# Gated attention and linear attention on one core: waits ordered by expected arrival, gate rows by DMA, a serial DMA queue in the build-time scheduler, the last round in two halves

## The chip, the cores and the metric

One core of one Trainium2 chip. The time is the device time of one execution in microseconds (us). The span is the time from the first to the last instruction in the profile; it is about 2 us shorter than the time (677.7 against 679.8 us in before's profiled run). All kernels below gave correct results.

## The reference

In short (both attentions are named here and not written out):

```python
def reference(A_x, A_wqkv, A_wo, B_x, B_wqkv, B_wo, gate_w):   # x: 1 x 2048 x 512, bf16
    x = A_x
    g = sigmoid((x * gate_w).sum(-1, keepdims=True))
    a = softmax_attention(x, A_wqkv, A_wo)      # branch A: 32 heads of 16, 2048 x 2048 scores
    b = linear_attention(x, B_wqkv, B_wo)       # branch B: phi(t) = where(t > 0, t+1, exp(t)) + 1e-6
    return g * a + (1 - g) * b
```

## The kernel before

The kernel schedules itself while it is built. A list scheduler holds a modelled duration for each operation and decides the order on each of the five engines; the instructions are then emitted in that order with semaphore waits. TensorE (PE) computes score blocks into PSUM banks (`ps<-Qz,KT`, three matmuls a group). Two of the three banks go to ScalarE (ACT), which takes the exponential of 128x1024 elements (`P<-ps`, 695 of them). The third goes to VectorE (DVE), which makes an approximate exponential by bit operations (`Z<-ps`, with shifts on DVE and GpSimd). PE multiplies both with V (`ps<-P,Vc`, `ps<-Z,Vc`: PV). Branch B and the projections are woven in between. Branch B's own exponentials on ACT write `eb` (32 of them); its normalised output (`OBn` in the program, `wA` in the profiles) is transposed by DMA (`xnat<-wA`) before the output matmuls read it. At the end of a round the attention output is transposed and normalised into `OAT`, which the output matmuls also read.

How waits are attached (the first of the list ends on the instruction, the others on EventSemaphore instructions ahead of it):

```python
    def add(self, fn, deps=(), inc=True, dma_sem=None):     # class _Eng
        waits = []
        for d in deps:
            if d is None:
                continue
            # ... semaphore and value of d; skipped if already waited for
                waits.append((sem, val))
```

How a DMA is modelled: the issue holds SP for 60 ns and the data land a fixed latency later, however many DMAs stand before it.

```python
        def dma(E, o, i, sem, total, lat, ..., issue=60.0):
            start = max(E.free, _avail(E, reads, writes))
            E.free = start + issue
            fin = start + lat
```

The loads at the start, the gate, and V's blocks:

```python
        for t in range(1, NQC):
            for cc in range(NCC):
                dma(SP, xT[...], x2[...], semXT[t], ..., transpose=True, issue=1300.0)     # 12 transposes
            # ... one weight load after t == 1
        dma(SP, gwc[:], gate_w.rearrange("(cc p) -> p cc", p=128), semG, 16, 3000.0, ...)  # 1 KB
...
            # a block of V: one eviction, then two scaled copies on GpSimd
            yield dv(607, lambda: nc.vector.tensor_copy(Vc[:, 0, vs, :, :, 0:16], src), [r_bank[b]], [r_V[vs]])
            for k in range(1, NTERM):
                yield po(690, lambda k=k: nc.gpsimd.tensor_scalar(Vc[:, k, vs]..., COEF[k], ...), [r_V[vs]], [r_V[vs]])
...
        def t_gate():
            yield po(900, lambda: nc.gpsimd.tensor_copy(gwr, gwc[:]...to_broadcast(...)), [r_gw], [r_gwr])
            # ... gate matmuls, sigmoid ...
            for a in range(4):          # gate rows: a strided copy per 32 partitions
                yield dv(150, lambda ...: nc.vector.tensor_copy(gnat[32 * a:32 * (a + 1), :], src), [r_ge], [r_gnat])
```

The softmax here doesn't subtract the row's maximum and nothing guards it: scores larger than these inputs give would overflow.

## Time and profile before

| | before |
|---|---|
| time, median of 3 runs | 680.0 us (679.25 to 680.65) |
| span of the profiled run | 677.7 us |
| first exponential starts / last one ends | 9.93 / 669.47 us |
| median distance between starts of exponentials | 904 ns |
| ACT time lost over that pace | 15.9 us |

The last row is the sum, over all consecutive exponentials, of the distance of their starts minus 904 ns (and minus 477 ns more where an `eb` activation lies between them). With the same exponentials at the same pitch, the time can fall only if such losses go, or if the head before the first exponential or the tail after the last gets shorter. The profile lines that carry this are in the prediction.

### The profile page before, as it was taken

The numbers are of one execution on the slowest core, as the hardware profiler recorded it, in microseconds if no ns is written. First come the engines' busy times: TensorE is split into PE (matmuls) and PEld (weight loads), VectorE is DVE, ScalarE is ACT, GpSimd is POOL, SyncE is SP. The second block draws the span as 40 slices with busy tenths as digits, with TensorE's granted clock in tenths as the row PEclk, the third lists the DMA queues.
The fourth block names the chain that finished last, engine by engine and source line by source line (L and its number), as shares of the span: only waits on it lengthen the run. The fifth ranks groups of instructions, "written<-read, shape, count | busy, mean of one in ns | idle before, by whom it ended". The sixth has DMA issues, their size and how long they took to land.

```text
span 677.7 us, 24102 instructions
## 1 busy us (share of the span) xinstructions
PE 667.5 (98%) x9886; PEld 203.2 (30%) x9886; DVE 607.9 (90%) x1062; ACT 658.2 (97%) x734; POOL 550.1 (81%) x611
## 2 busy tenths in 40 slices
PE   8999999999999999999999999999999999999998
PEld 4322233323223232222333322232332332222222
DVE  6999999998899998999899888899998988899996
ACT  5899999999999999999999999999999999999995
POOL 3767878888878888888897888898788997887882
PEclk9999999999999999999999999999999999999999
DMA  6430001200000000000002000001020021000000
GB/s 133 135 89 8 4 2 35 69 9 3 2 10 1 10 2 2 10 2 2 12 3 65 10 10 1 10 18 22 7 34 9 14 48 31 17 16 11 26 17 32
DMA packets 27963, 15.96 MB, mean 24 GB/s; under 512 B 19792, under 2 KB 26832, under 8 KB 27856
## 3 DMA queue, kind: packets, MB, share of 16 engines
q1 hardware_dynamic: 26512, 13.91, 8.1%
q8 instruction: 79, 1.29, 0.8%
q10 hardware_dynamic: 1344, 0.52, 0.3%
q14 instruction: 28, 0.23, 0.1%
HBM read 6.69 MB, written 2.10 MB: 13 GB/s over the span
## 4 chain that ended last, share of the span: by engine, by line
PE 77%; ACT 13%; issue 5%; DVE 4%; DMA 0%; POOL 0%; ACTq 0%; DVEq 0%; POOLq 0%
PE ps L371 59%; PE ps L377 18%; ACT P L771 11%; DVE Z L685 2%; ACT eb L1056 1%; DMA xnat<-wA 0%; DVE T L1021 0%; DVE gnat L1013 0%; DVE QT L957 0%; DVE wA L1163 0%; PE ps L899 0%; DVE Z L749 0%; DVE OAT L1048 0%; POOL Z L739 0%; DVE rec L1040 0%
## 5 line engine op out<-in xcount | busy, mean ns | idle before, releaser
L771 ACT ACTIVATE P<-ps 128x1024 bf16<-128x1024 f32 x695 | 645.6, 1118 | 5.9 <-PE ps L371 5.8
L739 POOL TENSOR_TENSOR Z<-Z,mcon 128x512 int32<-128x512 int32 x465 | 480.0, 1056 | 81.9 <-DVE Z L685 49.4
L685 DVE TENSOR_SCALAR Z<-ps 128x512 int16<-128x512 f32 x659 | 441.2, 684 | 53.3 <-PE ps L371 45.7
L371 PE MATMUL ps<-Z,Vc 128*17 128x512 bf16 x1977 | 282.4, 382 | 0.2
L371 PE MATMUL ps<-Qz,KT 32*128 32x512 bf16 x2048 | 272.2, 384 | 3.4 <-DVE Z L685 1.0
L371 PE MATMUL ps<-P,Vc 128*17 128x512 bf16 x1389 | 250.1, 383 | 0.2
L371 PEld LDWEIGHTS ps<-Qz,KT 32*128 32x128 bf16 x2048 | 68.5, 91 | 259.1 <-ACT P L771 235.1
L371 PEld LDWEIGHTS ps<-Z,Vc 128*17 128x17 bf16 x1977 | 63.8, 88 | 79.4 <-issue 52.3
L749 DVE TENSOR_SCALAR Z<-Z 128x1024 int16<-128x1024 int16 x195 | 81.2, 433 | 0.2
L371 PEld LDWEIGHTS ps<-P,Vc 128*17 128x17 bf16 x1389 | 56.3, 88 | 55.4 <-issue 40.7
L371 PE MATMUL ps<-warm 128*32 128x512 bf16 (+15 forms) x600 | 62.5, 327 | 1.2 <-DVE dummy L420 1.2
L377 PE MATMUL ps<-xT,wA 128*32 128x512 bf16 (+1 forms) x528 | 43.9, 376 | 0.1
L1057 POOL TENSOR_SCALAR eb<-eb 128x512 f32<-128x512 f32 x32 | 20.1, 629 | 15.6 <-ACT eb L1056 9.1
L988 POOL TENSOR_SCALAR Vc<-Vc 128x576 bf16<-128x576 bf16 x32 | 21.6, 675 | 6.9 <-DVE Vc L985 3.5
L371 PEld LDWEIGHTS ps<-warm 128*32 128x32 bf16 (+1 forms) x600 | 20.3, 96 | 18.8 <-issue 12.4
L1021 DVE STREAM_TRANSPOSE T<-ps 128x512 f32<-128x512 f32 x32 | 22.6, 708 | 2.5 <-PE ps L377 2.3
L377 PE MATMUL ps<-wA,xnat 128*32 128x512 bf16 x256 | 22.6, 382 | 1.7 <-DVE wA L1163 1.7
L1044 POOL TENSOR_TENSOR T<-T,rg 128x256 bf16<-128x256 f32 x31 | 19.5, 630 | 5.7 <-DVE Z L749 2.7
L377 PE MATMUL ps<-phiK,xnat 128*32 128x512 bf16 x256 | 23.1, 383 | 0.0
L377 PE MATMUL ps<-wA,OAT 128*32 128x512 bf16 x256 | 22.5, 382 | 0.0
L1056 ACT ACTIVATE eb<-ps 128x512 f32<-128x512 f32 x32 | 22.5, 702 | 0.0
L377 PE MATMUL ps<-wB,xT 128*32 128x512 bf16 x256 | 22.4, 381 | 0.0
(79 smaller groups left out, 279.2 us busy)
## 6 DMA issues: line engine op xcount, KB each, us to landing
Qz<-QT SPq DMA_DIRECT2D x120, 16.0 KB, 1.8
wA<-in_A_wqkv_dram SPq DMA_DIRECT2D x4, 384.0 KB, 4.6
wB<-in_B_wqkv_dram SPq DMA_DIRECT2D x4, 384.0 KB, 3.3
xnat<-in_A_x_dram SPq DMA_DIRECT2D x3, 512.0 KB, 3.7
out_dram<-outt SPq DMA_DIRECT2D x12, 128.0 KB, 1.7
wA<-in_A_wo_dram SPq DMA_DIRECT2D x1, 512.0 KB, 3.6
wA<-in_B_wo_dram SPq DMA_DIRECT2D x1, 512.0 KB, 4.6
out_dram<-wA SPq DMA_DIRECT2D x4, 128.0 KB, 1.8
```

Source lines behind the costliest of these rows:

```text
L371: return lambda: nc.tensor.matmul(o, lhsT=l, rhs=r, start=start, stop=stop, skip_group_check=sg)
L377: h = nc.tensor.matmul(o[32 * j:32 * j + 32], lhsT=l[:, 32 * j:32 * j + 32], rhs=r, start=start, stop=stop, skip_group_check=True)
L685: return C(DV, OPP, 533 * n + 74, lambda: nc.vector.tensor_scalar(o, i, ZB, 0.0, op0=ALU.add, op1=ALU.max), [r_bank[b] for b in bks], r_Z[ ...
L739: return C(PO, 400, 70 + 484 * n, lambda: nc.gpsimd.tensor_tensor(Z[:, z, 0:512 * n].bitcast(I32), Z[:, z0, 0:512 * n].bitcast(I32), mcon[ ...
L749: return C(DV, 450 if hot else 300, 69 + 134 * n, lambda: nc.vector.tensor_scalar(Z[:, z, 0:512 * n], Z[:, z0, 0:512 * n], float(m), None, ...
L771: return C(AC, 500, 427 * n + 49, lambda: nc.scalar.activation(P[:, slot, 0:512 * n], bank(b0, n), ACT.Exp, scale=ESC), [r_bank[b0 + k] fo ...
L988: yield po(690, lambda k=k: nc.gpsimd.tensor_scalar(Vc[:, k, vs].rearrange("p a b c -> p (a b c)"), Vc[:, 0, vs].rearrange("p a b c -> p ( ...
L1021: yield dv(607, lambda: nc.vector.transpose(T1[:, a, :], bank(7)), [r_bank[7]], [r_T1[a]])
L1044: yield E(340 if r == NR - 1 else 640, lambda k=k: (nc.vector if r == NR - 1 else nc.gpsimd).tensor_tensor(dst_[:, k], src[:, k, :, 0:16], ...
L1056: yield ac(480, lambda: nc.scalar.activation(eb[:, i, :], bank(b), ACT.Exp), [r_bank[b]], [r_eb[i]])
L1057: yield po(640, lambda: nc.gpsimd.tensor_scalar(eb[:, i, :], eb[:, i, :], 1.0 + 1e-6, 0.0, op0=ALU.min, op1=ALU.max), [r_eb[i]], [r_eb[i]])
```

## The change

Its intent: put the wait that is expected to end last on the instruction itself, where it is cheaper (in before's profile a score group of three matmuls ended at the earliest 460 ns after its last arrival with that wait on the instruction, and 547 ns with it on an EventSemaphore); take the four gate-row copies off VectorE; make the scheduler see that DMAs of one queue follow each other (in before's profile eight Qz copies of 16 KB held SP for 5.49 us), so that it issues urgent ones earlier; and normalise the last attention round in two halves, so that the first output tiles start sooner. Some twenty scheduler constants are tuned anew with it. Cut to its core:

```diff
-        for d in deps:
-            if d is None:
-                continue
+        for d in sorted([d for d in deps if d is not None], key=lambda d: -d.fin if isinstance(d, _Ev) else 0.0):
@@ constants (cut)
-    BACK = 1005.06
-    SHB = 4
+    BACK = 980.186
+    SHB = 2
@@ DMA model
+        q_free = [0.0]
+            if E is SP and occ:
+                q_free[0] = max(q_free[0], start) + occ
+                fin = q_free[0] - occ + lat
...
+                fin = dma(SP, ..., occ=1100.0 if tr or c.name[0] in 'WX' else 650.0)
@@ gate rows
             for a in range(4):
-                src = ge[32 * a:32 * (a + 1), :, :].rearrange(...)[:, :, a]
-                yield dv(150, lambda a=a, src=src: nc.vector.tensor_copy(gnat[32 * a:32 * (a + 1), :], src), [r_ge], [r_gnat])
+                yield ("DMA", gnat[32 * a:32 * (a + 1), :], gp[32 * a:32 * (a + 1), 16 * a:16 * (a + 1)], semGN, 64, 2500.0, [r_ge], [r_gnat], False, a == 0)
@@ last round
+            if r == NR - 1:
+                for hf in range(2):
+                    # transpose, reciprocal, two multiplies, transpose back, each on 256 columns
+                    yield ("FLAG", lambda hf=hf: flags.add(("oatl", hf)))
```

More of the change, by code (lines that the diff above doesn't have):

```diff
@@ L29, with __init__ @@
 class _Ev:
-    __slots__ = ("E", "idx")
-    def __init__(self, E, idx):
+    __slots__ = ("E", "idx", "fin")
+    def __init__(self, E, idx, fin=0.0):
         self.E = E
         self.idx = idx
+        self.fin = fin
 class _Eng:
@@ L159, in bass_gated_mix__mha_block__linear_attn_block__prompt_kernel @@
     SWITCH = 100.0
-    FILL = 0.704
+    FILL = 0.7
     HOT = 32.85
-    BACK = 1005.06
-    SHB = 4
+    BACK = 980.186
+    SHB = 2
     why = [None]
@@ L166, in bass_gated_mix__mha_block__linear_attn_block__prompt_kernel @@
     PLATE = -199.667
-    SLK = 43.219
-    DSL = 900.0
-    STICK = 45.888
+    SLK = 88.975
+    DSL = 843.776
+    STICK = 65.578
     OPP = 400
     FDL = 60
-    DENS = 0.581
+    DENS = 0.743
     AGE = 300.0
+    PEP = 148.771
+    PVD = 216
     MZ = 0.0
     MZD = 0.0
-    HOLD = 74.192
+    HOLD = 109.508
     NACT = 4
-    BIAS = 141.142
-    KEYW = 32.578
-    PVW = 1365.46
-    DTOL = 44.045
-    TTOL = 38.407
-    PKR, MTR, PQR, PQS, FR = 0.500, 9.56, 12.93, 1.804, 0.0
-    KR, KS, QR = 7.15, 1.60, 4.00
+    BIAS = 82.599
+    KEYW = 7.061
+    PVW = 511.557
+    DTOL = 186.116
+    TTOL = 37.928
+    PKR, MTR, PQR, PQS, FR = 0.404, 8.73, 13.55, 1.600, 0.0
+    KR, KS, QR = 5.59, 1.48, 4.00
     NB = 2
@@ L248, in bank @@
             return ps[:, 512 * b:512 * (b + n)]
-        PE = _Eng("pe", SEM("s_pe"), 150.0)
+        PE = _Eng("pe", SEM("s_pe"), PEP)
         AC = _Eng("act", SEM("s_act"), 115.0)
@@ L277, in bass_gated_mix__mha_block__linear_attn_block__prompt_kernel @@
         r_OAT = [[R(f"OAT{t}_{q}") for q in range(NQC)] for t in range(NT8)]
+        r_OATL = [R("OATL0"), R("OATL1")]
         r_eb = [R(f"eb{i}") for i in range(2)]
@@ L306, in deps_of, with emit @@
             return deps
-        def emit(E, dur, fns, reads=(), writes=(), name=""):
+        def emit(E, dur, fns, reads=(), writes=(), name="", more=0.0):
             if callable(fns):
@@ L312, in emit @@
             E.free = start + dur
-            fin = start + dur + E.pipe
+            fin = start + dur + E.pipe + more
             deps = deps_of(E, reads, writes)
@@ L320, in emit @@
                 ev = E.add(fn, deps if k == 0 else (), inc=(k == len(fns) - 1))
+                ev.fin = fin
                 if first is None:
@@ L333, in emit, with dma @@
             LOG.append((start, E.name, dur, name))
-            RLOG.append((E.name, dur, E.pipe, [(d.E.name, d.idx) if isinstance(d, _Ev) else ("dma", id(d.sem), d.val) for d in deps if d is not None],
+            RLOG.append((E.name, dur, E.pipe + more, [(d.E.name, d.idx) if isinstance(d, _Ev) else ("dma", id(d.sem), d.val) for d in deps if d is not None],
                          ev.idx, name, cur_mode[0] if E is PE else None))
             return fin
-        dma_eng = {}
-        def dma(E, o, i, sem, total, lat, reads=(), writes=(), transpose=False, noncontig=False, name="dma", issue=60.0):
+        q_free = [0.0]
+        def dma(E, o, i, sem, total, lat, reads=(), writes=(), transpose=False, noncontig=False, name="dma", issue=60.0, occ=0.0):
             start = max(E.free, _avail(E, reads, writes))
@@ L392, in bass_gated_mix__mha_block__linear_attn_block__prompt_kernel @@
         q_fill = [0] * NQZ
+        semGN = SEM("s_gn")
         semOB = [SEM(f"s_ob{i}") for i in range(2)]
@@ L479, in t_free @@
             return max([r_bank[b].tw] + list(r_bank[b].tr.values())) + LAT
-        DMIN = 3
+        DMIN = 4
         def ready(r, kb):
@@ L828, in after @@
                 STATS["pv"] = STATS.get("pv", 0) + 1
-            return C(PE, prio, 216, fns, reads, [r_bank[7]], after, f"PV{r} {[(w['kb'], w['name']) for _, _, w in wave]}", "col",
+            return C(PE, prio, PVD, fns, reads, [r_bank[7]], after, f"PV{r} {[(w['kb'], w['name']) for _, _, w in wave]}", "col",
                      0.25 * len(wave))
@@ L865, in pe_step @@
         def pe_step(n, cols, fns, reads, writes, mode="col"):
-            return ("OP", PE, n * (cols / 2.4 + 4), fns, reads, writes, mode)
+            return ("OP", PE, n * (cols / 2.4 + PVD - 212.5), fns, reads, writes, mode)
         def pe_thin(b, fns, reads):
@@ L1009, in t_gate @@
             yield dv(650, lambda: nc.vector.reciprocal(gt[:], ge[:]), [r_ge], [r_gt])
-            yield po(200, lambda: nc.gpsimd.tensor_scalar(ge[:], gt[:], -1.0, 1.0, op0=ALU.mult, op1=ALU.add), [r_gt], [r_ge])
+            gp = ge[:].rearrange("p q c -> p (q c)")
+            yield po(200, lambda: nc.gpsimd.tensor_scalar(gp.rearrange("p (a u) -> p a u", a=4), gt[:].rearrange("p q (c a) -> p a (q c)", a=4),
+                                                          -1.0, 1.0, op0=ALU.mult, op1=ALU.add), [r_gt], [r_ge])
             for a in range(4):
-                src = ge[32 * a:32 * (a + 1), :, :].rearrange("p q (c a2) -> p (q c) a2", a2=4)[:, :, a]
-                yield dv(150, lambda a=a, src=src: nc.vector.tensor_copy(gnat[32 * a:32 * (a + 1), :], src), [r_ge], [r_gnat])
+                yield ("DMA", gnat[32 * a:32 * (a + 1), :], gp[32 * a:32 * (a + 1), 16 * a:16 * (a + 1)], semGN, 64, 2500.0, [r_ge], [r_gnat], False, a == 0)
             yield ("FLAG", lambda: flags.add("gate"))
@@ L1020, in aout, with tr_half @@
             yield ("WAIT", lambda: r < 2 or ("aout", r - 1 - a) in flags)
-            yield dv(607, lambda: nc.vector.transpose(T1[:, a, :], bank(7)), [r_bank[7]], [r_T1[a]])
+            def tr_half(hf):
+                cs = slice(256 * hf, 256 * (hf + 1))
+                return dv(341, lambda: nc.vector.transpose(T1[:, a, cs], bank(7)[:, cs]), [r_bank[7]], [r_T1[a]])
+            if r == NR - 1:
+                yield tr_half(0)
+            else:
+                yield dv(607, lambda: nc.vector.transpose(T1[:, a, :], bank(7)), [r_bank[7]], [r_T1[a]])
             def free_acc():
-                st["acc_free"] = True
+                st["acc_free"] = r < NR - 1
                 st["pv_round"] = r + 1
@@ L1033, in aout @@
             k0 = ks[0]
+            if r == NR - 1:
+                for hf in range(2):
+                    cs, gs = slice(256 * hf, 256 * (hf + 1)), slice(8 * hf, 8 * (hf + 1))
+                    if hf:
+                        yield tr_half(1)
+                    sv = T1[:, 1, cs].rearrange("p (q d) -> p q d", d=32)
+                    yield dv(115, lambda sv=sv, gs=gs: nc.vector.reciprocal(rec[:, 1, gs], sv[:, :, 16]), [r_T1[1]], [r_rec[1]])
+                    yield dv(70, lambda gs=gs: nc.vector.tensor_tensor(rg[:, c, 1, gs], rec[:, 1, gs], gt[:, qc, gs], ALU.mult), [r_rec[1], r_gt], [r_rg[c]])
+                    yield dv(210, lambda sv=sv, gs=gs, cs=cs: nc.vector.tensor_tensor(
+                        T2[:, c, cs].rearrange("p (q h d) -> p h q d", h=2, d=16)[:, 1], sv[:, :, 0:16],
+                        rg[:, c, 1, gs].unsqueeze(2).to_broadcast([128, 8, 16]), ALU.mult), [r_T1[1], r_rg[c]], [r_T2[c]])
+                    yield dv(341, lambda cs=cs: nc.vector.transpose(OAT[:, t8, 512 * qc:512 * (qc + 1)][:, cs], T2[:, c, cs]), [r_T2[c]], [r_OATL[hf]])
+                    yield ("FLAG", lambda hf=hf: flags.add(("oatl", hf)))
+                return
             src = T1[:, k0:k0 + n, :].rearrange("p a (q d) -> p a q d", d=32)
@@ L1040, in aout @@
             yield dv(155 + 17 * n, lambda: nc.vector.reciprocal(rc, src[:, :, :, 16]), rT1, rr)
-            E = dv if r == NR - 1 else po
-            yield E(70 if r == NR - 1 else 230 + 25 * n, lambda: (nc.vector if r == NR - 1 else nc.gpsimd).tensor_tensor(rgc, rc, gv, ALU.mult), [*rr, r_gt], rrg)
+            yield po(230 + 25 * n, lambda: nc.gpsimd.tensor_tensor(rgc, rc, gv, ALU.mult), [*rr, r_gt], rrg)
             for k in range(n):
-                yield E(340 if r == NR - 1 else 640, lambda k=k: (nc.vector if r == NR - 1 else nc.gpsimd).tensor_tensor(
+                yield po(640, lambda k=k: nc.gpsimd.tensor_tensor(
                     dst_[:, k], src[:, k, :, 0:16], rgc[:, k].unsqueeze(2).to_broadcast([128, 16, 16]), ALU.mult),
@@ L1069, in t_load @@
         def t_load(k, n, dst, src, sem, lat, wr, flag):
-            yield ("DMA", dst, src, sem, 16 * n, lat, [now()], wr, False, k == 0)
+            yield ("DMA", dst, src, sem, 16 * n, lat + 1000.0, [now()], wr, False, k == 0)
             if k == n - 1:
@@ L1187, in rd @@
                 kind, i = seqk[k]
-                return [r_xn[qb], r_woB] if kind == "b" else [r_OAT[i][qc], r_woA]
+                return [r_xn[qb], r_woB] if kind == "b" else [r_OATL[qbl // 2] if tail and i == NT8 - 1 else r_OAT[i][qc], r_woA]
             for k0, k1 in ((0, 2), (2, 4), (4, 6), (6, 7)):
                 yield pe_step(k1 - k0, 512, [f(k) for k in range(k0, k1)], sum((rd(k) for k in range(k0, k1)), []), [r_bank[b]])
-            yield ("WAIT", lambda: ("oat", NT8 - 1, qc) in flags)
+            yield ("WAIT", lambda: (("oatl", qbl // 2) if tail else ("oat", NT8 - 1, qc)) in flags)
             yield pe_step(1, 512, [f(7)], rd(7), [r_bank[b]])
@@ L1200, in t_final @@
                 yield ("WAIT", lambda: qb < 2 or ("f", qb - 2) in flags)
-            if tail and qbl % 2 == 1:
+            if tail and qbl != 2:
                 yield ac(480, lambda: nc.scalar.copy(ot, bank(b)), [r_bank[b]], [r_ot])
@@ L1452, in bass_gated_mix__mha_block__linear_attn_block__prompt_kernel @@
                 _, o, i, sem, tot, lat, rd, wr, tr, chk = c.fns[1]
-                fin = dma(SP, o, i, sem, tot, lat, reads=rd, writes=c.writes, transpose=tr, name=c.name)
+                fin = dma(SP, o, i, sem, tot, lat, reads=rd, writes=c.writes, transpose=tr, name=c.name, occ=1100.0 if tr or c.name[0] in 'WX' else 650.0)
                 if not chk:
```

## The prediction

> **What bounds the kernel now.** I read the page's busy shares first, then the groups, then distances between starts on ScalarE (ACT), then a timeline around each long distance.
>
> ```profile
> PE 667.5 (98%) x9886; PEld 203.2 (30%) x9886; DVE 607.9 (90%) x1062; ACT 658.2 (97%) x734; POOL 550.1 (81%) x611
> L771 ACT ACTIVATE P<-ps 128x1024 bf16<-128x1024 f32 x695 | 645.6, 1118 | 5.9 <-PE ps L371 5.8
> PEld ps L371 <- ACT P L771: 238.2, 602, 1.2
> ```
>
> PE and ACT both look full. The third line (from the waits) decides between them: 602 times PE's weight loads wait for an exponential (L771), 238 us in all, while ACT waits for PE only 5.8 us. So PE follows ACT, through the score banks that an exponential frees. PE's 98% includes padding (matmuls on `warm`). A duration of 1118 ns is no cost either: consecutive exponentials overlap. From start to start the trace has 904 ns as the median; 461 of the 661 distances between two exponentials lie within 900 to 919 ns. An `eb` activation (32 of them) adds 477 ns.
>
> The first exponential starts at 9.9 us, the last ends at 669.5, and 8.2 us follow to the end of the span (677.7). Taking 904 or 477 ns off every distance leaves 15.9 us of lost ACT time in these 659.5 us. The page's 5.9 us is only the part in which ACT is visibly empty. With no loss at all the span would be 677.7 - 15.9 = 661.8 and, with the 2.3 us between span and measured time (680.0 - 677.7), the time 664.1. That is 2.3% under the present one, so a gain over 2% (under 666.4 us) needs nearly all the losses.
>
> I traced each late exponential to the PE group whose semaphore released it, and that group to its own last wait. The 15.9 us divide so: 8.0 us in 184 small delays where PE was busy with earlier work (44 ns each); 3.5 us in 13 cases where the score group waited for VectorE (DVE); 4.0 us in 7 cases where PV matmuls were late to free a P or bank slot; the rest are crumbs. Two cases of the second kind are large, and the change addresses both.
>
> ```profile
> 63.12 2.13 DVE L1013 COPY gnat<-ge 32x16 f32<-32x16 f32 x4
> 66.30 0.13 PEld L371 LDWEIGHTS ps<-Qz,KT 32*128 32x128 bf16 x3 [1.19 <-ACT P L771]
> 66.33 0.39 PE L371 MATMUL ps<-Qz,KT 32*128 32x512 bf16 x3 [1.04 <-DVE Z L685]
> 66.76 1.02 ACT L771 ACTIVATE P<-ps 128x1024 bf16<-128x1024 f32 x1 [0.76 <-PE ps L371]
> ...
> 552.65 3.67 SPq L352 DMA_DIRECT2D Qz<-QT  x5
> 556.36 5.19 SPq L348 DMA_TRANSPOSE xnat<-wA  x3
> 559.63 0.69 DVE L1163 TENSOR_TENSOR wA<-ps,wA 128x512 bf16<-128x512 f32 x1 [2.06 <-DMA xnat<-wA]
> 561.50 1.02 ACT L771 ACTIVATE P<-ps 128x1024 bf16<-128x1024 f32 x1 [1.66 <-PE ps L371]
> ```
>
> Columns are start, duration, engine, line, operation. Upper block: four gate-row copies hold DVE for 2.1 us where the kernel's scheduler planned 4 x 150 ns; the DVE half of a score group is late, its bank is not free, ACT starts 0.91 us late. Lower block: the issue queue on SP works through Qz copies first, so the transposes of OBn start at 556.36; DVE stands 2.06 us for one of them, ACT starts 1.77 us late.
>
> [...] the first wait in the kernel's list ends up on the instruction, the others on EventSemaphores ahead of it. [...] A three-matmul score group ends at the earliest 460 ns after its last semaphore arrives if that wait is on the matmul, and 547 ns if it is on the EventSemaphore: 87 ns dearer. [...] So "expected last placed first" moves the real wait onto the instruction.
> [...] the first two gate copies took 0.72 and 0.97 us and ended 29 and 35 ns after a GpSimd shift; the last two, with GpSimd idle, 0.17 us each.
> [...] 550.8 to 561.5 us: eight Qz copies took 5.5 us to issue, about 0.69 each; the scheduler counted 60 ns.
>
> **The change part by part.** The kernel schedules itself while it is built, so the new constants reorder PE nearly everywhere; I compared the two instruction streams. Work is nearly the same: 695 exponentials in both (before, one was half size), 2048 score matmuls, 3364 PV matmuls instead of 3366, 199 padding groups instead of 202. Shifts move slightly from DVE (195 to 187) to GpSimd (465 to 471: 6 x 1.06 = 6 us on an engine that is 81% busy, so free).
>
> - Gate rows by DMA: four DVE copies leave (2.1 us of DVE), four small SP copies come, some 0.7 us of issue each, ahead of Qz copies that have time. On the path: the 0.9 us stall at 66.8. **-0.9**.
> - Serial queue: in the new stream seven OBn transposes go out in a row before the last eight Qz copies (before: five), and the one transpose behind them is read only by the output matmuls, over 100 exponentials later; the DVE multiply that waited has 11 exponentials, about 10 us, after its transpose's issue. The stall at 561.5 goes. **-1.8**.
> - Wait order: before, the last arrival was on an EventSemaphore for 38 score groups and 26 PV groups on PE (64 x 87 ns = 5.6 us) and 66 times on GpSimd [...]. Only a part was on ACT's path: of the 13 score groups, 11 without the two large ones, 11 x 0.087 = **-0.95**. PV and shift latency works through the 8.0 us of PE delays. Score groups of four rows, which are slower and alternate with groups of two, fall from 24 to 4. I take an eighth of the 8.0 us for both: **-1.0**, the softest term.
> - Start: PE's first 81 groups stand in the same order in both programs, and the stalls at 22.2, 24.7 and 26.3 us lie in them (0.44 + 1.54 + 0.71 = 2.7 us).
>
> ```profile
> 24.23 0.40 PE L371 MATMUL ps<-P,Vc 128*17 128x512 bf16 x4
> 24.68 1.02 ACT L771 ACTIVATE P<-ps 128x1024 bf16<-128x1024 f32 x1 [1.42 <-PE ps L371]
> ```
>
>  There ACT waits for a free P slot, that is for PV, which waits for V of the second block. They stay: 0. The two stalls at 35.1 and 38.2 (0.6 + 0.3) fall where the order differs; I count half: **-0.45**.
> - Last round in halves:
>
> ```profile
> 670.41 0.72 DVE L1021 STREAM_TRANSPOSE T<-ps 128x512 f32<-128x512 f32 x1 [2.27 <-PE ps L377]
> 671.16 0.25 DVE L1040 RECIPROCAL rec<-T 128x16 f32<-128x16 f32 x1
> 671.45 0.17 DVE L1042 TENSOR_TENSOR rg<-rec,gt 128x16 f32<-128x16 f32 x1
> 671.66 0.42 DVE L1044 TENSOR_TENSOR T<-T,rg 128x256 bf16<-128x256 f32 x1
> 672.12 0.71 DVE L1048 STREAM_TRANSPOSE OAT<-T 128x512 bf16<-128x512 bf16 x1
> ```
>
>  The old chain takes 2.43 us from 670.41. A transpose of half width saves 256 columns at about 1 ns, so half chain = 0.45 + 0.25 + 0.17 + 0.30 + 0.45 with gaps, an estimate of 1.8 us. The first half is out 0.6 us earlier; the second, on the same engine, ends near 1.8 + 1.6 = 3.4, 1.0 later than before. In return its two output tiles are copied side by side by DVE and ACT, where before two copies followed each other on each (1.29 us on DVE), and fewer groups stand before the transpose. That is worth about as much as it costs, less the full-size last exponential (about 0.3). Sum **0**.
>
> Total -0.9 - 1.8 - 0.95 - 1.0 - 0.45 = -5.1: 680.0 - 5.1 = 674.9.
>
> **The rivals.** (a) ACT was the bound all along and stalls are only displaced: retuned constants make a few new ones of 0.5 to 1.5 us, as the old ones did, and the time stays at 678 to 680. For it: 8.0 us come from 184 scattered delays that no item names. Against it: the two large stalls have causes that the change takes out. (b) The retuned schedule cuts most of the 8.0 us as well: about 668 to 670. For it: PE has slack, an unhindered score-to-score loop with two other groups takes 866 ns against 904. Against it: the counts of such groups between two score groups are nearly as before (two groups 455 times, now 444; three 169, now 176; four or more 38 in both). (c) Wrong guesses: in 61 score groups the new order expects DVE last and puts ACT on the EventSemaphore; if ACT ends last there, each pays 87 ns, at most 5 us, most of it hidden. That makes 677 or so. (d) The new gate copies delay the third Qz load: its 8 copies have tens of exponentials of time, so I give it nothing.
>
> **Range and chances.** The named stalls (2.7 us) are nearly sure; the others may be twice or none, or be offset by new stalls of 1 to 2 us. So 671 to 679 should hold it 8 times in 10. Faster by over 2% would need 13.6 of 15.9 us: 0.03. Slower by over 2% would need 13.6 us of new stalls with the same work: 0.01.
>
> **What would show it.** Right: ACT's exponential pitch still 904 ns; no wait of DVE on the OBn transposes; no copies into `gnat` on DVE and no gap near 66 us; the three stalls near 22 to 26 us unchanged; last arrivals on EventSemaphores well under 38 and 66; the tail after the last exponential 8 us within 0.5. Wrong: a changed pitch, new ACT gaps over 0.5 us after 40 us, ACT losses outside 9 to 13 us, or a tail that moves by over 1 us.

The 460 and 547 ns come from the times of semaphore updates in before's profile and hold for score groups of three matmuls; that the 26 PV groups cost as much is the author's estimate. The cost on GpSimd is not shown: in before's profile, where GpSimd was idle and DVE's arrival came last, a shift started 68 ns after it with that wait on the shift (median of 29) and 133 ns after it with the wait on an EventSemaphore (median of 27), but its own semaphore update came 1227 ns after it in both (medians). The -1.0 us, which counted on it in part, is the author's estimate. Score groups of four matmuls are called slower: by the same measure they end at the earliest after 470 ns, those of three after 460, those of two after 452. The 1 ns a column of a transpose can be checked in the profile after: 0.45 us for 256 columns and 0.71 for 512.

## The result, and the profile after

Ratios here and below are the mean time of one kernel's runs over that of the other's in the same rounds, so not quite the ratio of the medians quoted.

| | before | after |
|---|---|---|
| time, median of 4 runs | 680.33 us (679.25 to 682.12) | 676.09 us (675.38 to 676.89) |
| ratio | | 0.9936, 95% interval 0.9911 to 0.996: same within 2% |
| span of the profiled run | 677.7 us | 674.2 us |
| ACT time lost | 15.9 us | 13.2 us |

The predicted time was 674.9 us (range 671 to 679). From the page of the kernel after and its table of waits (engine, line, what it waited for: us, times, longest), the three lines that answer to the first three of before:

```profile
PE 660.7 (98%) x9813; PEld 202.2 (30%) x9839; DVE 603.4 (89%) x1053; ACT 658.3 (98%) x735; POOL 559.4 (83%) x617
L778 ACT ACTIVATE P<-ps 128x1024 bf16<-128x1024 f32 x695 | 645.5, 1117 | 3.9 <-PE ps L377 3.7
PEld ps L377 <- ACT P L778: 232.0, 579, 0.8
```

The regime is unchanged: PE still waits for exponentials (579 times) far more than ACT for PE (3.7 us). The median pitch is still 904 ns (451 of 661 distances within 900 to 919 ns).

The timeline after, at the two places of the large stalls (start, duration, engine, line, operation):

```profile
61.41 7.46 ACT L778 ACTIVATE P<-ps 128x1024 bf16<-128x1024 f32 x8
...
551.80 12.94 ACT L778 ACTIVATE P<-ps 128x1024 bf16<-128x1024 f32 x14
555.24 4.94 SPq L358 DMA_DIRECT2D Qz<-QT  x8
556.33 0.67 DVE L1190 TENSOR_TENSOR wA<-ps,wA 128x512 bf16<-128x512 f32 x1
560.23 1.26 SPq L354 DMA_TRANSPOSE xnat<-wA  x1
```

Each ACT line is an unbroken row of exponentials across the place where ACT stood for 0.91 us (66.8) and 1.77 us (561.5) before. There is no gate copy on DVE, and DVE's multiply at 556.33 waits for no transpose: the one transpose left behind the Qz copies is read later.

To see where the 3.5 us of span come from, I cut the profiled runs at the starts of the same exponentials. Two experiments that are told below stand beside them: before with only the two stalls and the wait order changed, and after with the gate weights loaded early.

| from - to | before | after | difference | before, three edits | after, gate weights early |
|---|---|---|---|---|---|
| span's start - exponential 41 | 49.98 | 49.72 | -0.26 | 50.07 | 48.32 |
| 41 - 61 | 19.56 | 18.94 | -0.62 | 18.59 | 18.94 |
| 61 - 501 | 417.56 | 416.70 | -0.86 | 417.30 | 416.70 |
| 501 - 601 | 95.53 | 93.91 | -1.62 | 93.85 | 93.66 |
| 601 - 695 | 86.10 | 86.09 | -0.01 | 86.09 | 86.10 |
| 695 - span's end | 8.98 | 8.80 | -0.18 | 9.02 | 9.11 |
| sum | 677.71 | 674.16 | -3.55 | 674.92 | 672.83 |

The gate copies lie in the second row, the late transpose in the fourth. At the start the stall at 25 us is longer in this profile than in before's. From the timeline after:

```profile
22.38 0.61 POOL L1001 COPY T<-gwc 128x512 bf16<-128x512 bf16 x1 [1.23 <-DMA gwc<-in_gate_w_dram]
23.07 1.47 POOL L995 TENSOR_SCALAR Vc<-Vc 128x576 bf16<-128x576 bf16 x2
24.60 0.40 PE L377 MATMUL ps<-P,Vc 128*17 128x512 bf16 x4 [0.98 <-POOL Vc L995]
25.05 5.80 ACT L778 ACTIVATE P<-ps 128x1024 bf16<-128x1024 f32 x6 [2.48 <-PE ps L377]
```

Read upwards: ACT stands 2.48 us for PE; PE stands for GpSimd's scaling of V (L995); GpSimd stood 1.23 us for the load of the gate weights `gwc` before it began their copy, and that scaling started 0.69 us after the copy. In all twelve profiles in which V's terms are tracked together the scaling starts 0.69 to 0.70 us after the copy, whether GpSimd had stood or not.

In before's profile the same copy did not wait:

```profile
21.79 0.61 POOL L994 COPY T<-gwc 128x512 bf16<-128x512 bf16 x1
```

That need not be the change's doing, as programs with one and the same start show both: among the five profiles that have before's own start (before and experiments 2, 5, 6 and 7) GpSimd stands 0 to 1.63 us for this load, the stall at 25 us is 1.54 to 2.96 us, and exponential 41 starts at 49.35 to 50.12 us. Where GpSimd did not stand (before, experiments 2 and 3) the stall was 1.54 to 1.56 us. So the -0.26 us of the first row lie within the spread of single profiles; from exponential 41 to the end the difference is -3.29 us, and -2.88 us for the three edits.

### The profile page after: what moved, and what is told of

The parts are those of the page before. It is cut to its first block, busy times and chain, and to the rows that moved or that the text cites. A ratio compares the mean times of both kernels' runs of the same rounds, so it can differ in the third digit from the quotient of the medians.

```text
span 674.2 us, 23975 instructions
## 1 busy us (share of the span) xinstructions
PE 660.7 (98%) x9813; PEld 202.2 (30%) x9839; DVE 603.4 (89%) x1053; ACT 658.3 (98%) x735; POOL 559.4 (83%) x617
## 4 chain that ended last, share of the span: by engine, by line
PE 50%; ACT 31%; issue 12%; SPq 2%; DVE 2%; POOL 1%; DMA 1%; ACTq 0%; DVEq 0%; POOLq 0%
PE ps L377 39%; ACT P L778 30%; PE ps L383 10%; SPq L354 2%; DVE Z L692 1%; ACT eb L1083 1%; POOL Z L746 1%; DMA gwc<-in_gate_w_dram 1%; DVE Z L756 0%; POOL Vc L995 0%; SPq L358 0%; ACTq L1495 0%; DVE OAT L1059 0%; DVE wA L1176 0%; DVE T L1031 0%
## 5 line engine op out<-in xcount | busy, mean ns | idle before, releaser
L746 POOL TENSOR_TENSOR Z<-Z,mcon 128x512 int32<-128x512 int32 x471 | 488.0, 1061 | 64.4 <-DVE Z L692 50.4
L377 PE MATMUL ps<-Z,Vc 128*17 128x512 bf16 x1974 | 272.5, 382 | 0.5 <-DVE Z L756 0.3
L377 PE MATMUL ps<-P,Vc 128*17 128x512 bf16 x1390 | 245.0, 383 | 1.0 <-POOL Vc L995 1.0
L377 PEld LDWEIGHTS ps<-Z,Vc 128*17 128x17 bf16 x1974 | 60.9, 88 | 69.1 <-issue 44.2
L756 DVE TENSOR_SCALAR Z<-Z 128x1024 int16<-128x1024 int16 x187 | 77.3, 433 | 0.0
L377 PE MATMUL ps<-warm 128*32 128x512 bf16 (+16 forms) x529 | 55.9, 326 | 4.7 <-issue 2.4
L995 POOL TENSOR_SCALAR Vc<-Vc 128x576 bf16<-128x576 bf16 x32 | 21.7, 679 | 6.0 <-DVE Vc L992 2.3
L383 PE MATMUL ps<-xT,wB 128*32 128x512 bf16 x256 | 22.3, 382 | 0.0
L1085 DVE SCALAR_TENSOR_TENSOR phiK<-ps,eb 128x512 bf16<-128x512 f32 x32 | 21.7, 678 | 0.2 <-POOL eb L1084 0.2
```

Source lines behind the costliest of these rows:

```text
L377: return lambda: nc.tensor.matmul(o, lhsT=l, rhs=r, start=start, stop=stop, skip_group_check=sg)
L383: h = nc.tensor.matmul(o[32 * j:32 * j + 32], lhsT=l[:, 32 * j:32 * j + 32], rhs=r, start=start, stop=stop, skip_group_check=True)
L746: return C(PO, 400, 70 + 484 * n, lambda: nc.gpsimd.tensor_tensor(Z[:, z, 0:512 * n].bitcast(I32), Z[:, z0, 0:512 * n].bitcast(I32), mcon[ ...
L756: return C(DV, 450 if hot else 300, 69 + 134 * n, lambda: nc.vector.tensor_scalar(Z[:, z, 0:512 * n], Z[:, z0, 0:512 * n], float(m), None, ...
L1085: yield dv(607, lambda: nc.vector.scalar_tensor_tensor(dst_ap, bank(b), 1e-6, eb[:, i, :], op0=ALU.max, op1=ALU.add), [r_bank[b], r_eb[i]] ...
```

## The experiments

All ran for five rounds in three calls, each with its own runs of the kernel before (medians 681.03, 680.52 and 681.66 us). Two things about those runs have to be known to read the ratios. First, of the 33 runs of before in these calls, 19 had a mean granted clock of 0.997 and 14 a clock of 1.000, and in each call the former were 1.5 to 2.2 us slower (means 681.86, 681.42 and 682.07 against 679.80, 679.97 and 679.87 us). Second, where I give a "clean" mean it is that of the runs with a clock of 0.999 or 1.000, about 679.9 us for before.

**1. The changed kernel without the sort.** All streams are the same, only the waits stand in their old order.

```diff
-        for d in sorted([d for d in deps if d is not None], key=...):
+        for d in [d for d in deps if d is not None]:
```

> The changed kernel with its waits in the old order; the instruction streams of all engines are the same as in the changed kernel, only the placing of waits differs. Theory (wait order is a small part): last arrivals on EventSemaphores go back from 23 to about 60 score groups or fewer and from 3 to about 25 PV groups; ACT's lost time grows by 0.2 to 1.0 us, the time is 676.3 to 677.3 us, ratio to the kernel before 0.994 to 0.996. Rival (wait order is the change's main gain): 679 us or more, ratio 0.998 to 1.000.

Measured: 676.2 us (675.92 to 677.04), ratio 0.9932 (0.9915 to 0.995), span 674.1: as the changed kernel. What the sort brings is below what these runs resolve.

**2. The kernel before with the sort alone.**

```diff
-        for d in deps:
+        for d in sorted([d for d in deps if d is not None], key=lambda d: -d.fin ...):
```

> The kernel before with the new wait order alone, all streams else unchanged. Theory: 0.2 to 1.0 us faster, ratio 0.9985 to 0.9997, with the gaps at 66.8 and 561.5 us still in the trace. Rival (wait order is the main gain): 3 to 4 us faster, ratio 0.994 to 0.9955.

Measured: 680.76 us (678.99 to 682.95), ratio 0.9998 (0.9975 to 1.0021), clean mean 679.74. Nothing again. By the semaphore records the sort did part of its work: of GpSimd's shifts with two waits, 40 had their last arrival, DVE's, on an EventSemaphore before, and none has now; of the score groups it is 30 instead of 38 (23 in the changed kernel), since the modelled order of arrival is not always the real one. ACT's losses show why it is worth so little: the small delays by DVE's late arrivals nearly vanish (0.82 to 0.15 us), but those under "PE busy with earlier work" rise from 8.05 to 9.23 us, and the total only falls from 15.9 to 15.5.

**3. The sort reversed**, so that the wait expected first is on the instruction and the real one on an EventSemaphore.

```diff
-... key=lambda d: -d.fin if isinstance(d, _Ev) else 0.0)
+... key=lambda d: d.fin if isinstance(d, _Ev) else 0.0)
```

> The changed kernel with the order reversed: of several waits the one expected last is placed last, so nearly every real wait falls on an EventSemaphore (some 440 score groups wait for ACT there at 87 ns each, 38 us of added latency on PE). Theory (latency of a score group is hidden while ACT still has the other bank pair to work on, and a loop with two other groups has 40 ns of slack): most is hidden, 1 to 5 us slower than the changed kernel, 677 to 681 us, ACT pitch still 904 ns as a median. Rival (the wait sits on the loop that sets the pace): 440 x 87 ns = 38 us slower, about 714 us, ACT pitch near 990 ns.

Measured: 683.65 us (682.48 to 684.15), ratio 1.0039 (1.0021 to 1.0057): 7.6 us by the medians over the changed kernel, more than the 1 to 5 us expected; the median pitch stayed at 904 ns. The last arrival is now on an EventSemaphore for 461 score groups instead of 23; the earliest end of such a group after it is again 547 ns against 460. All on the path, 438 x 87 ns would be 38 us; about a fifth came through (less if GpSimd's waits, also moved, are part of it). ACT's losses rise from 13.2 to 19.5 us. So the cost of a wait's place on PE (87 ns a score group) is real, but about four fifths of it are hidden, and before's order was mostly right already.

**4. The kernel before with only the new scheduler constants.**

```diff
-    BACK = 1005.06        # and all the others of the diff above
+    BACK = 980.186
```

> The kernel before with all the new scheduler constants (and DMIN 4), nothing else of the change. The schedule differs nearly everywhere. Theory (constants shift the small delays about but do not lower their sum): 679 to 682 us, ratio 0.998 to 1.003, and the lost ACT time within 14 to 18 us. Rival (the retuned constants are the main gain): 677 us or less, ratio 0.995 or less, lost ACT time under 13 us.

Measured: 679.98 us (679.49 to 680.43), ratio 0.9986 (0.9967 to 1.0005), clean mean 679.94. The order is other nearly everywhere, the late transpose no longer stalls ACT, and still nothing is gained: a stall of 3.4 us at 25.5 us (GpSimd stood 1.96 us for the gate weights in this profile) and one of 0.95 us at 61 us, at the gate copies, are in the trace. The new order also gives ACT two more exponentials than before, 697, which at 904 ns cost about as much, 1.8 us, as the lost transpose stall had.

**5. The kernel before, schedule held, gate rows by DMA.** VectorE's four copies become tiny memsets of scratch, so that nothing else moves.

```diff
-                yield dv(150, ... nc.vector.tensor_copy(gnat[32 * a:32 * (a + 1), :], src), [r_ge], [r_gnat])
+                yield dv(150, lambda a=a: nc.vector.memset(gscr[:, a:a + 1], 0.0), [r_ge], [r_gscr])
+                # and four DMAs gnat <- gp on SP
```

> The kernel before with its schedule held fixed; only the gate rows change: four SP DMAs (each after the first Qz copies) bring them, and VectorE's four copies are replaced by tiny memsets of scratch, so that all other streams stay as they were. Theory (the stall at 66.8 us is worth its 0.9 us): 679.4 +- 0.4, ratio about 0.9987, and no ACT gap over 0.3 us near 66 us. Rival (a stall taken out is given back at the next late score group): 680.3, ratio 1.000, with ACT's losses elsewhere up by 0.9 us.

Measured: 680.22 us (678.53 to 681.13), ratio 0.999 (0.9973 to 1.0007); clean mean 678.99, 1.0 under before's. In the profile the stretch from exponential 41 to 61 fell from 19.56 to 18.58 us. The theory's size is right, though the interval of the ratio includes no gain.

This profiled run fell among those with a clock of 0.997 and shows where its clock was lower. Stretches of time with the busy time of each engine; after them the granted PE clock, the DMA share and GB/s; before first, then this run:

```profile
560.00:562.00 2.00, 1.53 (x22) 0.46 (x22) 2.00 (x4) 0.50 (x1) 2.00 (x3) 1.00 0.23 47
562.00:564.00 2.00, 2.00 (x32) 0.56 (x29) 1.43 (x3) 1.98 (x3) 0.66 (x1) 1.00 0.12 26
564.00:566.00 2.00, 2.00 (x29) 0.49 (x30) 1.65 (x4) 2.00 (x3) 0.04 (x1) 1.00 0.00 0
```

```profile
560.00:562.00 2.00, 1.68 (x22) 0.49 (x22) 2.00 (x4) 0.65 (x1) 2.00 (x3) 0.96 0.30 62
562.00:564.00 2.00, 2.00 (x18) 0.39 (x15) 0.74 (x2) 1.40 (x2) 0.47 (x1) 0.50 0.06 11
564.00:566.00 2.00, 2.00 (x22) 0.34 (x19) 1.03 (x2) 1.36 (x2) 0.00 (x0) 0.69 0.00 0
```

And the timelines of that run, ACT's and PE's:

```profile
560.32 0.62 PE L379 MATMUL ps<-wA,xnat 128*32 128x512 bf16 x8 [1.75 <-DVE wA L1178]
561.35 2.10 ACT L774 ACTIVATE P<-ps 128x1024 bf16<-128x1024 f32 x2 [1.71 <-PE ps L373]
564.37 1.02 ACT L774 ACTIVATE P<-ps 128x1024 bf16<-128x1024 f32 x1 [0.92 <-PE ps L373]
565.66 1.94 ACT L774 ACTIVATE P<-ps 128x1024 bf16<-128x1024 f32 x2 [0.27 <-PE ps L373]
```

The stall at 561.5 us, which this kernel still has, leaves PE idle for 1.75 us. Here the clock was then at half (0.50 between 562 and 564 us), PE did 18 matmuls where it did 32, and ACT stood twice more, for 0.92 and 0.27 us. In the clock records the half clock here lasts 3.41 us, the full clock in the two main profiles lasts a whole number of times as long (672.4 us in before's are 197 times, 669.0 us in the changed kernel's 196), and it starts at other places of the span (at 6.8 and at 5.4 us). A stretch of this length, counted from the start of the full clock, is called a window here. With the time cut at the windows' ends, this run first, then before, then experiment 10:

```profile
558.43:561.84 3.41, 1.66 (x26) 0.45 (x22) 2.36 (x4) 1.70 (x3) 3.41 (x5) 1.00 0.32 66
561.84:565.25 3.41, 3.41 (x33) 0.59 (x29) 1.59 (x3) 2.44 (x3) 0.63 (x1) 0.50 0.08 16
```

```profile
556.32:559.73 3.41, 2.46 (x30) 0.66 (x26) 1.35 (x4) 3.41 (x4) 3.41 (x5) 1.00 0.43 89
559.73:563.15 3.42, 2.68 (x37) 0.81 (x37) 3.16 (x5) 1.76 (x3) 2.93 (x3) 1.00 0.19 38
```

```profile
23.85:27.26 3.41, 1.78 (x78) 1.11 (x76) 2.96 (x7) 0.93 (x1) 1.80 (x3) 1.00 0.31 122
27.26:30.68 3.42, 3.35 (x97) 1.52 (x89) 2.97 (x5) 3.33 (x5) 2.52 (x4) 1.00 0.37 120
```

Here the whole gap fell into one window, PE was busy for 1.66 us of it (the first number after the comma), and the next window ran at half clock. In before's profile the same gap, 1.69 us, fell across two windows and the clock stayed. In the 13 profiles with clock records (experiment 11's has none), from the first full clock to 9 us before the end, this is the only window in which PE was busy for under half and the only one followed by half clock; the next lowest is experiment 10's, 1.78 us, with none. In those last 9 us one window with 1.50 us (experiment 4) was not followed by half clock either, so half is where the two cases part here, not a measured threshold. A gap of 1.7 us falls whole into one window of 3.41 us in about half of all placements (an estimate, 1 - 1.7/3.41). The runs fit: before and the two kernels that keep this stall (experiments 2 and 5) had such a clock in 25 of 45 runs; the nine kernels without it and other than experiments 6 and 11 (the changed one included) in none of 52. Experiments 6 and 11 had it in 1 and 2 of 6 runs without this stall, for a reason that no profile shows.

**6. The kernel before, schedule held, the one late transpose earlier on SP's queue** (after three of the eight Qz copies).

```diff
+        SPL.insert(first + MOVE, SPL.pop(late))     # MOVE = 3
+        for E, go, dd, sem, _ in SPL:
+            E.add(go, dd, inc=False, dma_sem=sem)
```

> The kernel before with its schedule held fixed; only SP's issue order changes: the OBn transpose that VectorE stood for 2 us at 559.6 goes out after three of the eight Qz copies instead of after all. Theory: the stall of 1.8 us at 561.5 goes and the time falls to 678.5 +- 0.4, ratio about 0.9974. Rival (given back later): 680.3, ratio 1.000.

Measured: 677.97 us (677.62 to 680.0), ratio 0.9965 (0.995 to 0.998), span 675.9, 1.8 under before's. This is a little under the 678.1 to 678.9 expected. ACT's row of exponentials is unbroken around 561 us. The span gives the 1.8 us of the theory; the ratio gives more, since before's mean contains runs with a clock of 0.997 (5 of the 11 in this call, against 1 of 6 here). Clean, it is 679.97 - 677.96 = 2.0 us.

**7. Both edits and the sort in before's schedule.**

```diff
+   the diffs of experiments 2, 5 and 6 together
```

> Both of the above and the sorted waits in before's own schedule: what the named parts of the change are worth with no rescheduling. Theory: -0.9 -1.8 -0.2 (the sort alone gave 0.9998) = 677.4, ratio 0.9957; then about 1.3 us of the 4.2 that the change gave are left for the new schedule and the tail. If the named parts were all, 676.1 (0.9936). Rival (gains come from the new schedule only): 680.3.

Measured: 676.9 us (676.42 to 678.03), ratio 0.9947 (0.9932 to 0.9962), span 674.9, no run below a clock of 0.999. The three edits in the old schedule give 2.8 of the 3.5 us of span that the whole change gives. Nothing was given back later.

**8. The changed kernel with V's three terms tracked apart**, so that PV of the first term need not wait for GpSimd's scaling.

```diff
-         r_V = [R(f"V{p}") for p in range(NVQ)]
+         r_V = [[R(f"V{p}_{k}") for k in range(NTERM)] for p in range(NVQ)]
```

> The changed kernel with one thing more: the three scaled terms of V are tracked apart, so PV of the first term need not wait until GpSimd has scaled the others. It aims at the stalls on a free P slot at 21.5 to 26.2 us (3.25 us of ACT in the changed kernel). The scheduler reflows, so noise of about 1 us is expected. Theory (these stalls are on the path that sets the end and come from the V block's last terms): they shrink to under 1 us and the time is 673 to 674.5, ratio to before about 0.990. Rival (PV waits for V's own matmuls and eviction, not the scaling, or the loss is given back): 676, ratio 0.9936.

Measured: 677.04 us (676.62 to 677.46), ratio 0.9947 (0.9934 to 0.996). The theory failed: the stall at 25 us shrank to 1.1 us (at 23.1), but new ones came at 28.6 (1.0 us) and 36.1 us (1.6 us), and exponential 41 starts at 49.68 instead of 49.72 us. In this stretch the scheduler's new order gave the gain back. The longer time has another cause: the last exponential starts at 665.30 us, as in the changed kernel (665.36), and then 10.15 us follow instead of 8.80. From this run's timeline:

```profile
669.91 0.45 DVE L1060 STREAM_TRANSPOSE OAT<-T 128x256 bf16<-128x256 bf16 x1
670.64 1.04 PE L383 MATMUL ps<-wA,xnat 128*32 128x512 bf16 x16
671.50 1.04 PE L383 MATMUL ps<-wA,OAT 128*32 128x512 bf16 x16
672.59 0.59 ACT L1230 CAST wA<-ps 128x512 bf16<-128x512 f32 x1 [2.23 <-PE ps L383]
```

The last half is out at 670.36 us, but PE has 16 matmuls of branch B (`wA,xnat`) in front of the last ones that read it. Experiment 11 shows the same.

**9. The changed kernel, schedule held, the 1 KB of gate weights loaded early**, on ACT's queue instead of SP's.

```diff
-        dma(SP, gwc[:], gate_w..., semG, 16, 3000.0, writes=[r_gw], noncontig=True, issue=500.0)   # after 12 transposes
+        AC.add(gw_go, (), inc=False, dma_sem=semG)                                                # before them
```

> The changed kernel with its schedule held fixed; only the 1 KB load of the gate weights (gwc) is issued early on ScalarE's queue instead of on SP behind twelve transposes of x. In all traces so far that load lands at about 21.5 to 22.8 us, GpSimd[...] stands for it (1.23 us in the changed kernel), and the scaling of V's second block comes after it. Theory (that stand is what holds PV and so the 2.6 us ACT stall at 25 us; it is absolute, set by SP's queue, so starting sooner makes it longer): GpSimd's wait for gwc is 0, the stall at 25 us is 1.2 to 1.6 us, the time 674.8 +- 0.5, ratio to before about 0.9918. Rival (PV waits for V's own projection or x's transposes): the stall and the time stay at 676.1, ratio 0.9937.

Measured: 675.22 us (674.68 to 675.7), ratio 0.9907 (0.9891 to 0.9923); it is faster than before and than the changed kernel (experiment 10, the changed one but for its tail, had 676.32 in the same rounds, and none of its runs was as fast as the slowest here). The same lines as above, from this run's timeline:

```profile
20.44 0.60 POOL L1008 COPY T<-gwc 128x512 bf16<-128x512 bf16 x1
21.13 1.43 POOL L1002 TENSOR_SCALAR Vc<-Vc 128x576 bf16<-128x576 bf16 x2
23.21 0.39 PE L377 MATMUL ps<-P,Vc 128*17 128x512 bf16 x4
23.65 6.71 ACT L785 ACTIVATE P<-ps 128x1024 bf16<-128x1024 f32 x7 [1.74 <-PE ps L377]
```

GpSimd and PE wait for nothing in front of these lines any more; ACT's gap is 1.74 us instead of 2.48. It was expected at 1.2 to 1.6 (1.86 by the loss count): the rest of this stall is not the load, as in the profiles where GpSimd did not stand (1.54 to 1.56 us). That the load set the start shows in the other profiles as well. In the eight in which GpSimd stood for it, exponential 21 starts 8.31 to 8.42 us (once 8.66) after the copy of `gwc` starts, while the first exponential starts anywhere from 8.64 to 9.94 us. This profile's first exponential was early too (8.66 us). Against experiment 1 with the same head (8.64), exponential 21 comes at 29.30 instead of 30.51 us: 1.2 us, of which the order of waits, the other difference, can have little part by experiment 1.

**10. The changed kernel with the last round at full width**, all else the same up to there.

```diff
-            if r == NR - 1:
-                for hf in range(2):
-                    ...
+            # the common code for all rounds, on VectorE in the last one, as before
```

> The changed kernel with the last round normalised at full width as before; all streams are the same up to the last round. Theory of the prediction (halves give as much as they cost): the span's tail after the last exponential differs by less than 0.3 us, time 676.1 +- 0.4. Rival 1 (halves gain 0.5 to 1 us, as the tail of 8.24 to 7.7 us suggests): 676.6 to 677.1, ratio about 0.995. Rival 2 (halves cost): 675.5.

Measured: 676.32 us (675.78 to 677.74), ratio 0.9922 (0.9904 to 0.9939). From the start of the last exponential to the end it takes 8.94 us, against 8.80 with halves. From the timelines, the changed kernel's DVE first, this run's second:

```profile
666.98 0.45 DVE L1031 STREAM_TRANSPOSE T<-ps 128x256 f32<-128x256 f32 x1 [3.30 <-PE ps L377]
668.23 0.45 DVE L1059 STREAM_TRANSPOSE OAT<-T 128x256 bf16<-128x256 bf16 x1
...
669.80 0.45 DVE L1059 STREAM_TRANSPOSE OAT<-T 128x256 bf16<-128x256 bf16 x1
```

```profile
668.38 0.72 DVE L1033 STREAM_TRANSPOSE T<-ps 128x512 f32<-128x512 f32 x1 [3.31 <-PE ps L377]
...
670.09 0.71 DVE L1060 STREAM_TRANSPOSE OAT<-T 128x512 bf16<-128x512 bf16 x1
```

Halves: the first is out 1.70 us after the start of the chain, the second 3.27 us; full width: 2.42 us. A transpose of half the width took 0.45 us against 0.71 or 0.72. The gain and the cost nearly cancel, as estimated.

**11. The changed kernel with the old constants.**

```diff
-    BACK = 980.186        # and the others
+    BACK = 1005.06
```

> The changed kernel with all of the old scheduler constants: the counterpart of the run of before with only the new ones (which gave 0.9986). Theory (constants carry nothing; the two named stalls, -2.8 us in the run that held before's schedule, and the tail carry the change): 676.5 +- 1.0, ratio about 0.994 to 0.995. Rival (new constants cut ACT's losses by 1 us or more once the DMA model is right): 677.5 or more, ratio above 0.996.

Measured: 678.71 us (678.21 to 682.76), ratio 0.9971 (0.9947 to 0.9994), clean mean 678.52. The rival held: with the new structure the constants are worth 678.5 - 676.1 = 2.4 us (2.0 against the mean of experiment 10 in the same rounds), although alone (experiment 4) they were worth nothing. The trace shows two places: a stall of 1.2 us at 369.7 us, and the tail, 10.21 us instead of 8.80. In the tail:

```profile
671.28 0.45 DVE L1059 STREAM_TRANSPOSE OAT<-T 128x256 bf16<-128x256 bf16 x1
672.01 0.82 PE L383 MATMUL ps<-wA,xnat 128*32 128x512 bf16 x12
672.66 1.04 PE L383 MATMUL ps<-wA,OAT 128*32 128x512 bf16 x16
673.75 0.58 ACT L1229 CAST wA<-ps 128x512 bf16<-128x512 f32 x1 [2.01 <-PE ps L383]
```

The last half is transposed at 671.73 us, but PE then has 12 matmuls of branch B (`wA,xnat`), which needed no half, in front of the last `OAT` matmuls, so ACT's last copy starts 2.02 us after it; in the changed kernel it is 0.93 us. Halves cost if the order of the output matmuls does not fit them.

**12. Experiments 8 and 9 together, rescheduled.**

```diff
+   the diffs of experiments 8 and 9 together
```

> The early gate weights and V's terms tracked apart, rescheduled. With V's terms apart alone the stall at 25 us went, but two others (28.6 and 36.1 us) came and the time was 677.0. Theory (those two came from the same late loads): 674 to 675. Rival (the scheduler's reflow decides, and a stall taken out at the start comes back while x and V are still arriving): 675.5 to 677.

Measured: 676.7 us (676.1 to 677.39), ratio 0.9929 (0.9912 to 0.9946). The time is the rival's, but only half of its reason held. Stalls of 1.1 us at 24.2 and 1.6 us at 36.0 us are there, exponential 41 starts at 49.63. The first exponential came late in this profile, however (10.07 us): from it to exponential 41 it is 39.56 us, as in experiment 9 (39.66) and less than in the changed kernel (40.41). What takes the gain away is the tail, 10.39 us, with the same 16 matmuls of branch B ahead of the last `OAT` ones as in experiment 8. With a tail of 8.80 us it would be at about 675.1 us (an estimate, 676.7 - 1.6), which no run tests. The best kernel measured is that of experiment 9.

## Why the prediction was right or wrong

The time (674.9 predicted, 676.1 measured) and "same" were right, and so was the main mechanism: the kernel is a row of exponentials at a pitch of 904 ns, and the change removes two stalls from it. About half of the predicted gain, 2.4 of 5.1 us, was not right. The range of 671 to 679 us is wide enough to hold the result even with those terms at zero (677.3), so the time alone does not confirm the sum. One of the signs that were named for being wrong came, narrowly: ACT's losses are 13.2 us, outside 9 to 13. By its own steps:

- **Gate rows, -0.9**: right. 1.0 us in experiment 5.
- **Serial queue, -1.8**: right for the stall: 1.8 us of span in experiment 6. That the new DMA model is what takes it away is not shown. No run has the model alone; the stall is gone with the model and the old constants (experiment 11), but also with the new constants and the old model (experiment 4). SP, which the prediction has issuing from 550.8 to 561.5 us, issues without a break up to 558.9; it then waits 1.4 us for the third transpose's data. A side effect was not foreseen: in over half of before's runs the clock was 0.997 and the run 1.5 to 2.2 us longer, and in the one profile of a kernel with this stall and such a clock, the half clock follows the window with the stall. So the timed gain (4.2 us by the medians) is above that of the profiled spans (3.5).
- **Wait order, -0.95**: this step failed. It took eleven score groups at 87 ns (547 against 460) for fully on the path. Experiments 1 and 2 gave nothing measurable; in experiment 3 about a fifth of the added cost arrived. At that share, the fall from 38 to 23 such groups is worth 15 x 87 ns / 5 = 0.26 us.
- **PE's small delays, -1.0**: this step failed, as its mark "softest term" allowed. They were 8.0 us and are 8.5 us; the 61 - 501 stretch, where most of them lie, gained 0.86 us, of which the three edits in the old schedule already have 0.26.
- **Start, 0**: right as far as the profiles can tell (-0.26 us up to exponential 41, less than the spread between runs). That the stalls stay as they are did not show: the one at 25 us is 2.60 us instead of 1.54, while the first exponential came 0.62 us sooner, but profiles of before's own start have 1.54 to 2.96 us as well. The prediction took them for fixed. It named V of the second block as the cause, rightly, but did not see that V can in turn wait for a copy of the gate weights ahead of it on GpSimd, whose load is issued at 18.3 us behind twelve transposes (in the changed kernel's profile four of them held SP for 5.12 us and the other eight for 10.74, about 1.3 us each). In the profile that it was made from there was no such wait. Experiment 9 showed it.
- **Stalls at 35 and 38 us, -0.45**: this step failed. They are 0.55 + 0.30 us, before 0.60 + 0.30.
- **Tail, 0**: right, -0.18 us, with 1.70 and 3.27 us for 1.8 and 3.4 estimated. It rests on the retuned constants (experiment 11).

The failed terms sum to -2.4 us. In their place the profile shows about -0.6 us: of the -3.5 us, -2.8 are the two stalls and the sort (experiment 7), -0.2 is the tail, and the rest goes to the new schedule; this rest is a difference of single profiles and no run isolates it. Rival (a), that stalls are only displaced, was wrong for the two large ones and right for the small ones. Rival (b) did not show (8.0 us of PE delays became 8.5), nor did (c).

That the clock dips come from this stall rests on one profile of a dip, on the windows of the others, and on the counts of runs; it is well supported, not shown for each run.

## What to carry to other kernels

Count a stall in full only where the bound engine visibly stands; many small delays of an engine that runs ahead of it pass only in part (here about a fifth), and removing some uncovered others (in experiment 2 the delays by DVE's late arrivals fell from 0.82 to 0.15 us and those under PE's earlier work rose from 8.05 to 9.23). When an instruction near the start is late, follow it back past the engine to the load behind it: work that nobody needs yet can hold up work that everybody needs if it stands ahead of it on the same engine (here GpSimd's copy of the gate weights, which stood 1.23 us for its load ahead of V's scaling), and one small DMA issued earlier was worth about 1 us here, against 4.2 us for the whole change. Hold the schedule fixed when you test one cause in a self-scheduling kernel, because each rescheduling moves other things by 1 to 2 us: in experiments 8, 11 and 12 the tail alone grew by 1.35 to 1.59 us, and a profile cut at fixed points is what shows it.
